# A linear attention and a gated layer on one core: w in pairs, halves summed before the column matmuls, w_out worked in place, and a new order

## The chip, the cores and the metric

The kernel runs on one core of a Trainium2 chip. The time is the device time of one execution in microseconds (us). The engines are named as the profile names them: PE (matmul) with PEld (its weight loads), DVE (vector), ACT (activation), POOL, and SP, which here only issues DMAs. Each engine takes its instructions in order.

## What is computed

The reference, cut to what matters. r, k, v, w have the shape (4, 8, 768, 48): batch, heads, steps, head size. The second part has 384 inputs and outputs and 1024 hidden columns.

```python
for t in range(S):
    cur = einsum('bhd,bhe->bhde', u * k[t], v[t])
    y[t] = einsum('bhd,bhde->bhe', r[t], state + cur)
    state = w[t][..., None] * state + einsum('bhd,bhe->bhde', k[t], v[t])
x = y.transpose(0, 2, 1, 3).reshape(B * S, H * D)
h = x @ w_in
e = exp(h - max(h)); sm = e / (sum(e) + 1e-9)
solu = h * sm
mu, var = mean(solu), mean((solu - mean(solu)) ** 2)
out = ((solu - mu) / sqrt(var + 1e-6) * g_ln) @ w_out
```

## The kernel before

The 768 steps are cut into 6 chunks of 128, and there are 4 batches, so there are 24 units of work (chunk, batch), each 128 tokens with all 8 heads. Units 0 to 3 are the first chunk. A unit goes through some thirty stages, and each stage is a small function that issues a few instructions on one engine. The text `ORDER` lists all stages of all units as words; the program goes through the words once and issues each, and a wrapper (`InOrder`) keeps every engine in that order. A word is a stage, a unit, and where there is a choice a letter: a for ACT, v for DVE, g for POOL. So `hq3a` squares for unit 3 on ACT. `ORDER` is therefore the order of PE, DVE, ACT, POOL and of SP's DMAs.

The stages by their words:

- `ldw`, `ldk`, `ldr`, `ldv`: SP loads 128x8x48 floats of an input, 192 KB in rows of 192 bytes. `ldwin`, `ldwout`, `small` load the weights and the two rows u and g_ln.
- `lw` (ACT): log of w. `cum` (PE): running sums of it, in `cum_ps`. `exp` (ACT): their exponentials in place. `et` (DVE): the decay over the whole chunk. `kp` (DVE): k and r times the decays.
- `p`, `q`, `qa`, `dg`, `dv`: the term with u: r times k, times u, summed per head (`qa` adds halves first on POOL), times v. `vb` makes v bf16.
- `kt` (PE) transposes `kp`, `kr` copies it out. `M` (PE) gives the scores in `m_ps`, `m` copies them with the mask on DVE, or without it on ACT, and then `sel` masks on POOL.
- `Y` (PE) is the attention, with the dv term added by a matmul where the word ends in x, and otherwise in `y`, which copies it out. `X` (PE) transposes y, `xT` copies. `S` (PE) and `st` (DVE) renew the state, in all but the last chunk.
- `H` (PE): the hidden layer, 24 matmuls into `h_ps`. `e` (ACT): its exponential. `he` (DVE): h times e. `hq`: the square of he.
- `Oa` and `Ob` (PE): for each of 8 hidden slices a matmul of he with `w2` (384 outputs and a column for the mean), and a matmul with one column for the sum of e; `Ob` ends with 8 one-column matmuls for the sum of hq. The last unit is worked in other parts (`Oa23`, `Ob23`, `Oc23`).
- `sq`, `qm`, `lv`, `o`, `sto`: the variance, its root, the scaled output, and the store by SP.
- `win` casts w_in. `gw` scales w_out by g_ln into `gw`, `mean` takes its mean over the hidden dimension with 8 matmuls, `mean_sb` copies it, `wt` adds it to `gw` and gives `w2`. `dm` is a matmul on zeros that only keeps PE busy.

SP issues the loads far ahead: k with r, v and w have seven buffers each. PSUM gives two large tiles (cum, m, h) and four small ones (all others).

The masks are built on POOL: `uti_neg` and `uts` by a memset and a select, `ident` and `ident_f` by a helper (masks.py in the profile). In the order in which the program issues POOL's work, those of the helper are partly behind the first `p`.

Every call of an `InOrder` engine carries line 71 in the profile, the first call of each line 68, so instructions are told apart by their tiles.

Of the kernel before, what the change touches and what calls it, by code (L numbers as in the profile page):

```python
# [24 lines left out]
dm5 dm3 dm18 dm1 ldw0 ldr0 small dm16 dm8 ldk0 lw0 ldw1 ldr1 cum0 exp0 et0 lw1 rows cum1 ldk1 p0g ldw2 kp0 exp1 ubc kt0 p1g kr0v ldr2 M0 ldk2 ldv0 et1  # L25
kp1 lw2 m0a q0g kt1 kr1v ldwin2 cum2 q1g sel0 dg0 exp2 M1 dm10 et2 vb0a kp2 m1a ldwin1 ldv1 kt2 win2a dg1 dv0g kr2v win1a vb1a Y0 y0v sel1 ldwin0 M2
win0a dm6 X0 m2v dv1v ldwout0 dm4 p2g Y1 q2g S1 y1v ldwout1 qa2 gw1a gw0a dm2 X1 xT0v xT1v dg2 H0 H1 ldw3 e0 st1 S0 dm13 ldv2 gw4v gw6v gw3g he0 ldk3
gw5a dm12 dm17 ldw4 st0 gw7a ldr3 e1 ldk4 lw3 gw2g mean mean_sb:a vb2g ldw5 dv2g he1 Y2 ldr4 cum3 wt2g y2v exp3 lw4 et3 p3v hq0a wt3g cum4 wt1g X2 dm0
wt0g ldk5 dm9 ldr5 exp4 lw5 ldw6 wt4g kp3 S2 kt3 ldv3 cum5 st2 ldw7 wt7g ldv4 et4 kr3a xT2v wt6g ldr6 Oa0 kp4 p4v exp5 wt5g M3 q3v et5 m3a kt4 kr4v
ldk6 Oa1 kp5 hq1a H2 M4 q4g kt5 Ob0 ldv5 sel3 ldw8 lw6 vb3a e2 dg3 kr5a dv3g m4v sq0a dg4 vb4g dv4g p5g vb5g Ob1 ldr7 M5 lw7 ldk7 Y3x ldv6 he2 m5v qm0  # L30
q5g p6g y3a cum6 X3 xT3v sq1v Y4 qm1 exp6 y4v H3 lv0 lv1 et6 ldr8 X4 hq2v ldk8 kp6 Oa2 dg5 o0a xT4a dv5g p7g sto0 ldw9 S4 e3 S3 st4 st3 q6g H4 Y5 vb6g
q7g ldr9 o1a he3 kt6 lw8 S5 Ob2 e4 ldk9 y5v cum7 ldr10 he4 kr6a st5 X5 hq3a sq2a exp7 M6 Oa4 ldv7 ldk10 ldr11 Oa3 qm2 m6v cum8 ldv8 qa6 et7 xT5a sto1
dg6 ldr12 ldk11 lv2 kp7 qa7 Ob3 dv6g exp8 p8g ldw10 p9v kt7 et8 o2a dg7 sq3g kp8 H5 qm3 q8g hq4a lv3 ldv9 e5 ldw11 Y6x kr7v ldv10 p10g M7 vb7g o3v Ob4
ldw12 kt8 m7v y6a q10g lw9 X6 sq4v he5 cum9 xT6a qm4 ldk12 exp9 kr8a dg8 et9 dv7g Y7 hq5g H6 e6 sto2 kp9 Oa5 ldw13 kt9 y7v lv4 X7 dg10 q9g Ob5 kr9a
he6 vb8g ldv11 ldk13 dv8g ldr13 sq5a o4a M8 ldw14 hq6g m8v S7 M9 qm5 vb10g xT7a p11g ldv12 m9v lv5 Oa6 H7 dg9 st7 lw10 Y8 o5a e7 cum10 vb9g ldw15
exp10 Ob6 y8v he7 sq6g X8 sto3 et10 dv9g S6 kp10 ldk14 xT8a lw12 S8 q11g H8 lw11 lw13 cum11 st8 e8 dv10g st6 Oa7 qm6 kt10 Y9x p12g exp11 hq7v kr10a
# [12 lines left out]
e18 he18 dv20g kt21 exp22 Ob17 kr21a M20 X19 sq17g S17 qm17 m20a lv17 kp22 qa21 sel20 lw23 S18 xT19v sto14 o17a st17 hq18g M21 Oa18 ldk23 m21v kt22
cum23 H19 sto15 st18 exp23 kr22v vb21a kp23 dg21 dv21g sto16 Y20 Y21 vb22a M22 q22g S19 e19 m22a vb23g y20v X20 p23v st19 he19 q23g Ob18 kt23 xT20a  # L50
sq18v H20 qm18 kr23a sel22 M23 y21v lv18 o18a X21 dg22 hq19v xT21v Oa19 m23a dv22v dg23 sel23 Y22 Ob19 y22v e20 he20 H21 dv23g Y23 sto17 X22 sq19a
Oa20 y23v X23 qm19 lv19 hq20g o19a xT22v e21 xT23v H22 e22 he21 Ob20 sto18 hq21g sq20a qm20 lv20 H23 he22 Oa21 Oa22 sto19 Ob21 e23 hq22g sq21a o20v
qm21 lv21 Ob22 he23 hq23v Oa23 sto20 sq22v sq23a qm22 o21v Ob23 sto21 lv22 qm23 Oc23 o22v sto22 lv23 dm14 oz23v dm15 o23a stz23 dm7 sto23 dm11 dm19
# [25 lines left out]
def kernel(  # L79
# [38 lines left out]
    def load(name, src):  # L118
        def stage(i):
            c, b = units[i]  # L120
            L = live[i]
            if name in "kr":

                if "k_and_r" not in L:
                    L["k_and_r"] = io.tile([C, 2, H, 64], F32, tag="kr_in", name="kr_in")
                t = L["k_and_r"][:, "kr".index(name)]
            else:
                t = io.tile([C, H, 64], F32, tag=name + "_in", name=name + "_in")
            L[name] = t[:, :, :D]
            sp.dma_start(out=L[name], in_=src[b, :, c * C:(c + 1) * C, :].rearrange("h t d -> t h d"))  # L130
        return stage
# [16 lines left out]
    def load_w_out(half):  # L148
# [5 lines left out]
    nc.gpsimd.memset(uti_neg, -1.0)  # L154
    nc.gpsimd.affine_select(out=uti_neg, in_=uti_neg, compare_op=ALU.is_ge, fill=0.0, base=0,
                            pattern=[[1, C]], channel_multiplier=-1)
    uts = consts.tile([C, C], BF16)
    nc.gpsimd.memset(uts, 1.0)
    nc.gpsimd.affine_select(out=uts, in_=uts, compare_op=ALU.is_gt, fill=0.0, base=0,
                            pattern=[[1, C]], channel_multiplier=-1)  # L160
    ident = consts.tile([C, C], BF16)
    make_identity(nc, ident)
# [12 lines left out]
    lw_t = [consts.tile([C, H, 64], BF16, name=f"lw{j}") for j in range(NR)]  # L175
    kp_t = [consts.tile([C, 2, H, 64], BF16, name=f"kp{j}") for j in range(NR)]
    for j in range(NR):
        nc.vector.memset(lw_t[j][:, :, D:], 0.0)
# [407 lines left out]
    def part(stage, j):  # L586
        return lambda i: stage(i, j)
# [52 lines left out]
```

The softmax here doesn't subtract the row's maximum and nothing guards it: scores larger than these inputs give would overflow.

## Time and profile before

| what | value |
|---|---|
| median of 8 runs | 151.86 us (150.96 to 155.74) |
| the profiled execution | 151.5 us, of which the span from first to last instruction is 149.8 |
| PE busy | 138.7 us, 2154 matmuls |
| DVE, ACT, POOL busy | 128.6, 119.5, 122.8 us |
| DMA | 27.09 MB, 181 GB/s on average |
| inv_col column matmuls for e | 192, row mean 165 ns |
| one_col column matmuls for hq | 192, row mean 163 ns |
| hq on POOL, on DVE, on ACT | 14 of 1892 ns, 5 of 1043, 5 of 1068 |
| lw on ACT | 24 of 523 ns |
| w_in, w_out in chunks | landing after 5.3 and 8.6 us (median) |

A row of the profile gives the mean duration of one instruction. A matmul's duration includes its way through the array, in which the next one already runs; what it adds to PE's time is the distance between two starts. Busy shares are averages over the start, the bulk and the tail, which differ.

### The profile page before, as it was taken

The numbers are of one execution on the slowest core, as the hardware profiler recorded it, in microseconds if no ns is written. First come the engines' busy times: TensorE is split into PE (matmuls) and PEld (weight loads), VectorE is DVE, ScalarE is ACT, GpSimd is POOL, SyncE is SP. The second block draws the span as 40 slices with busy tenths as digits, with TensorE's granted clock in tenths as the row PEclk, the third lists the DMA queues.
The fourth block names the chain that finished last, engine by engine and source line by source line (L and its number), as shares of the span: only waits on it lengthen the run. The fifth ranks groups of instructions, "written<-read, shape, count | busy, mean of one in ns | idle before, by whom it ended". The sixth has DMA issues, their size and how long they took to land.

```text
span 149.8 us, 5293 instructions
## 1 busy us (share of the span) xinstructions
PE 138.7 (93%) x2154; PEld 109.7 (73%) x2156; DVE 128.6 (86%) x231; ACT 119.5 (80%) x232; POOL 122.8 (82%) x152
## 2 busy tenths in 40 slices
PE   5766899599999899999999999999999999999993
PEld 2244677377886787887878888878787878888780
DVE  7545778999999998999989989988899999997661
ACT  4446939898798979799898998798999798895651
POOL 3374983999989999998988999999798989975900
PEclk9999999999999999999999999999999999999999
DMA  5999999998989998989899999996989111011113
GB/s 99 197 221 321 391 297 203 205 213 172 217 194 199 205 221 170 232 167 236 197 213 240 217 201 229 205 261 135 239 201 255 42 57 53 7 53 57 48 50 117
DMA packets 104970, 27.09 MB, mean 181 GB/s; under 512 B 100329, under 2 KB 104562, under 8 KB 104946
## 3 DMA queue, kind: packets, MB, share of 16 engines
q1 hardware_dynamic: 104946, 26.75, 78.8%
q8 instruction: 17, 0.28, 0.7%
q14 instruction: 7, 0.06, 0.1%
HBM read 22.03 MB, written 4.72 MB: 179 GB/s over the span
## 4 chain that ended last, share of the span: by engine, by line
PE 72%; DVE 11%; DMA 5%; issue 4%; ACT 4%; SPq 2%; POOL 0%; POOLq 0%; DVEq 0%; ACTq 0%
PE o_ps L71 23%; PE h_ps L71 19%; PE kr_ps L71 8%; DMA kr_in<-in_k_dram 5%; PE cum_ps L71 5%; PE y_ps L71 4%; PE m_ps L71 4%; PE s_ps L71 4%; PE x_ps L71 3%; DVE kp L71 3%; DVE p L71 2%; SPq L71 2%; DVE he L71 1%; ACT cum_ps L71 1%; DVE y L71 1%
## 5 line engine op out<-in xcount | busy, mean ns | idle before, releaser
L71 PE MATMUL o_ps<-w,he 128*128 128x385 bf16 (+2 forms) x200 | 42.3, 315 | 0.3 <-ACT sq L71 0.3
L71 PE MATMUL h_ps<-xT,win_sb 128*128 128x128 bf16 x576 | 36.3, 220 | 0.1
L71 PEld LDWEIGHTS <-win_sb 128*128 128x128 bf16 x576 | 33.3, 98 | 0.8 <-issue 0.2
L71 DVE TENSOR_TENSOR he<-h_ps,e 128x1024 bf16<-128x1024 f32 x24 | 29.2, 1217 | 3.2 <-ACT e L71 3.2
L71 PE MATMUL o_ps<-inv_col,e 128*128 128x1 bf16 x192 | 31.1, 165 | 0.0
L71 ACT ACTIVATE e<-h_ps 128x1024 bf16<-128x1024 f32 x24 | 24.5, 1022 | 7.5 <-PE h_ps L71 7.4
L71 POOL TENSOR_TENSOR hq<-he 128x1024 bf16<-128x1024 bf16 x14 | 26.5, 1892 | 3.1 <-DVE he L71 2.1
L71 PEld LDWEIGHTS <-he 128*128 128x128 bf16 x208 | 19.7, 96 | 10.5 <-issue 0.3
L71 ACT ACTIVATE cum_ps<-cum_ps 128x772 f32<-128x772 f32 (+1 forms) x24 | 19.3, 803 | 5.7 <-PE cum_ps L71 5.6
L71 DVE TENSOR_TENSOR kp<-cum_ps,kr_in 128x768 bf16<-128x768 f32 x24 | 22.7, 947 | 0.2 <-ACT cum_ps L71 0.2
L71 POOL TENSOR_TENSOR q<-p,u_bc 128x384 bf16<-128x384 bf16 x23 | 21.2, 926 | 0.7 <-DVE p L71 0.5
L71 POOL TENSOR_TENSOR dv<-vb,dg 128x384 bf16<-128x384 bf16 x22 | 18.5, 845 | 3.6 <-DVE dg L71 1.7
L71 PEld LDWEIGHTS <-kp 128*128 128x128 bf16 x272 | 17.6, 102 | 4.5 <-DVE kp L71 2.5
L71 DVE TENSOR_TENSOR m<-m_ps,uts 128x1024 bf16<-128x1024 f32 x14 | 17.0, 1221 | 2.8 <-PE m_ps L71 2.6
L71 POOL TENSOR_TENSOR p<-kr_in 128x384 bf16<-128x384 f32 x18 | 18.4, 1026 | 1.1 <-DMA kr_in<-in_k_dram 1.1
L71 PEld LDWEIGHTS <-e 128*128 128x128 bf16 x192 | 18.3, 96 | 0.1
L71 PE MATMUL kr_ps<-ident,kp 128*128 128x128 bf16 x192 | 15.9, 230 | 2.1 <-DVE kp L71 2.1
L71 ACT COPY kr<-kr_ps 128x1024 bf16<-128x1024 bf16 x13 | 13.2, 1015 | 0.8 <-PE kr_ps L71 0.8
L71 PEld LDWEIGHTS <-kr 64*128 64x128 bf16 (+1 forms) x272 | 10.5, 98 | 4.5 <-DVE kr L71 2.2
L71 ACT ACTIVATE lw<-w_in 128x384 bf16<-128x384 f32 x23 | 11.7, 523 | 0.9 <-DMA w_in<-in_w_dram 0.9
L71 POOL TENSOR_SCALAR_AFFINE_SELECT m<-m 128x1024 bf16<-128x1024 bf16 x10 | 11.0, 1100 | 1.8 <-ACT m L71 1.8
L71 PE MATMUL m_ps<-kr 64*128 64x128 bf16 x192 | 10.2, 229 | 1.7 <-DVE kr L71 1.7
(93 smaller groups left out, 280.7 us busy)
## 6 DMA issues: line engine op xcount, KB each, us to landing
w_in<-in_w_dram SPq DMA_DIRECT2D x24, 192.0 KB, 3.7
kr_in<-in_r_dram SPq DMA_DIRECT2D x24, 192.0 KB, 3.6
kr_in<-in_k_dram SPq DMA_DIRECT2D x24, 192.0 KB, 4.3
v_in<-in_v_dram SPq DMA_DIRECT2D x24, 192.0 KB, 4.4
out_dram<-o SPq DMA_DIRECT2D x23, 192.0 KB, 3.2
win_f<-in_moe_w_in_dram SPq DMA_DIRECT2D x3, 512.0 KB, 5.3
wout_f<-in_moe_w_out_dram SPq DMA_DIRECT2D x2, 768.0 KB, 8.6
out_dram<-o SPq DMA_DIRECT2D x2, 96.0 KB, 1.7
```

The lines of the kernel that those rows point to most:

```text
L71: made = make(*args, **kwargs)
```

## The change

Seven things are changed.

1. w is held in pairs of units: one tile for two, and from unit 4 on one DMA (384 KB) loads both and one activation takes the log of both. `ldw5`, `lw5` and so on are gone from the order. The first four units are loaded and worked singly.
2. `gw` writes into `w2` itself, and `wt` adds the mean to it in place; the tile `gw` is gone. The 8 matmuls of the mean are in two halves (`meanA`, `meanB`).
3. A stage `es` adds slices 4 to 7 of e to slices 0 to 3, and then the sum of e takes 4 column matmuls, not 8. It is in the order for units 16 to 22 (POOL for 18 and 19, DVE for the others).
4. A stage `hs` does the same for hq, for units 18 to 22 (POOL for 20, DVE for the others).
5. The column matmuls of e for the second half are no longer between those of `Ob` but in a stage `Oe`, for units without `es`.
6. The four masks are built by POOL in order, ahead of all its other work.
7. The order is new as a whole, and for many stages the engine. Counts: hq 8 on POOL, 3 on DVE, 13 on ACT; kr 10 on ACT, 14 on DVE (13 and 11 before); m 12 and 12 (10 and 14); xT 11 and 13 (14 and 10); sel 12 (10); qa 9 (6); dv all on POOL; gw 1 on ACT, 4 on DVE, 3 on POOL (4, 2, 2); dm 16 (20).

The diff, cut. Of the order, its beginning and its end are shown.

```diff
 ORDER = """
-dm5 dm3 dm18 dm1 ldw0 ldr0 small dm16 dm8 ldk0 lw0 ldw1 ldr1 cum0 exp0 et0 lw1 rows cum1 ldk1 p0g ldw2 kp0 exp1 ubc kt0 p1g kr0v ldr2 M0 ldk2 ldv0 et1
-kp1 lw2 m0a q0g kt1 kr1v ldwin2 cum2 q1g sel0 dg0 exp2 M1 dm10 et2 vb0a kp2 m1a ldwin1 ldv1 kt2 win2a dg1 dv0g kr2v win1a vb1a Y0 y0v sel1 ldwin0 M2
-win0a dm6 X0 m2v dv1v ldwout0 dm4 p2g Y1 q2g S1 y1v ldwout1 qa2 gw1a gw0a dm2 X1 xT0v xT1v dg2 H0 H1 ldw3 e0 st1 S0 dm13 ldv2 gw4v gw6v gw3g he0 ldk3
-gw5a dm12 dm17 ldw4 st0 gw7a ldr3 e1 ldk4 lw3 gw2g mean mean_sb:a vb2g ldw5 dv2g he1 Y2 ldr4 cum3 wt2g y2v exp3 lw4 et3 p3v hq0a wt3g cum4 wt1g X2 dm0
+dm11 dm2 dm10 dm9 dm5 dm4 ldw0 lw0 cum0 ldk0 exp0 ldr0 et0 p0g ldw1 dm6 small dm13 dm0 lw1 rows kp0 ubc ldk1 q0g cum1 kt0 dm3 exp1 ldr1 ldw2 lw2 dm7
+ldk2 kr0v ldr2 ldv0 ldwin2 M0 ldwin0 et1 kp1 kt1 m0v ldwin1 ldv1 cum2 p1g kr1a M1 dg0 exp2 ldwout0 q1g vb0v dm14 dv0g m1a Y0x et2 ldw3 kp2 kt2 p2g y0a
+kr2v win0g win2a ldwout1 q2v dm15 sel1 vb1g ldv2 dg1 M2 win1a m2a S0 X0 ldr3 xT0v dv1g H0 st0 Y1 e0 dg2 y1v ldk3 sel2 X1 S1 xT1a he0 st1 gw3g gw2g
+gw5g gw1v lw3 gw0v gw6v H1 vb2g ldw4 hq0a dv2g cum3 e1 gw4v meanA he1 gw7a exp3 ldr4 meanB ldk4 et3 Y2x S2 ldv3 mean_sb:a wt3g kp3 ldr5 hq1a kt3 y2a
+p3v wt0g X2 wt2g lw4 ldk5 kr3v M3 wt1g cum4 wt7v q3v st2 ldv4 ldw6 m3a wt4g wt5g cum5 Oa0 wt6g Oa1 exp4 p4v exp5 et4 xT2a kp4 q4v et5 kt4 kp5 H2 ldr6
...
-Oa20 y23v X23 qm19 lv19 hq20g o19a xT22v e21 xT23v H22 e22 he21 Ob20 sto18 hq21g sq20a qm20 lv20 H23 he22 Oa21 Oa22 sto19 Ob21 e23 hq22g sq21a o20v
-qm21 lv21 Ob22 he23 hq23v Oa23 sto20 sq22v sq23a qm22 o21v Ob23 sto21 lv22 qm23 Oc23 o22v sto22 lv23 dm14 oz23v dm15 o23a stz23 dm7 sto23 dm11 dm19
+es20v xT22a hs19v lv18 Y23 H22 e21 y23v hq20g X23 he21 xT23v Ob19 o18a e22 he22 sq19a qm19 Oa20 hs20g es21v H23 lv19 o19a e23 Ob20 hq21v es22v Oa21
+sq20g hq22a qm20 Oa22 lv20 hs21v sto17 o20a Ob21 sq21v he23 hs22v hq23v Ob22 qm21 sq22v Oa23 sto18 sto19 lv21 sto20 qm22 sq23a Ob23 o21v lv22 qm23
+lv23 sto21 Oc23 o22v o23v sto22 oz23a dm12 stz23 dm1 dm8 sto23
 """
...
+            elif name == "w":
+                if i % 2 == 0:
+                    t2 = io.tile([C, 2, H, 64], F32, tag="w_in", name="w_in", bufs=4)
+                    for a in range(2):
+                        live[i + a]["w2_in"] = t2
+                        live[i + a]["w"] = t2[:, a, :, :D]
+                if i >= 4:
+                    sp.dma_start(out=L["w2_in"].rearrange("t a h d -> t (a h) d")[:, :, :D],
+                                 in_=src[b:b + 2, :, c * C:(c + 1) * C, :].rearrange("b h t d -> t (b h) d"))
+                else:
+                    sp.dma_start(out=L["w"], in_=src[b, :, c * C:(c + 1) * C, :].rearrange("h t d -> t h d"))
+                return
...
-    make_identity(nc, ident)
+    ident_f = consts.tile([KF, KF], F32)
+    for t, value, keep, fill in ((uti_neg, -1.0, ALU.is_ge, 0.0), (ident, 0.0, ALU.not_equal, 1.0),
+                                 (uts, 1.0, ALU.is_gt, 0.0), (ident_f, 0.0, ALU.not_equal, 1.0)):
+        pool.memset(t, value)
+        pool.affine_select(out=t, in_=t, compare_op=keep, fill=fill, base=0,
+                           pattern=[[1, t.shape[1]]], channel_multiplier=-1)
...
-            act.activation(out=gw[:, f, :], in_=wout_f[:, f, :], func=COPY, scale=gr[:, f:f + 1])
+            act.activation(out=w2[:, f, :DM], in_=wout_f[:, f, :], func=COPY, scale=gr[:, f:f + 1])
...
-        engine.tensor_add(out=w2[:, f, :DM], in0=gw[:, f, :], in1=mean_sb)
+        engine.tensor_add(out=w2[:, f, :DM], in0=w2[:, f, :DM], in1=mean_sb)
...
     def log_w(i):
-        L = live[i]
-        L["lw"] = lw_t[i % NR]
-        act.activation(out=L["lw"][:, :, :D], in_=L["w"], func=LN)
+        t = lw_t[i // 2 % (NR // 2)]
+        both = range(i, i + 2) if i >= 4 else range(i, i + 1)
+        for j in both:
+            live[j]["lw"] = t[:, j % 2]
+        if len(both) == 2:
+            act.activation(out=t.rearrange("t a h d -> t (a h) d")[:, :, :D],
+                           in_=live[i]["w2_in"].rearrange("t a h d -> t (a h) d")[:, :, :D], func=LN)
+        else:
+            act.activation(out=live[i]["lw"][:, :, :D], in_=live[i]["w"], func=LN)
...
-            pe.matmul(o_ps[:, DM + 1:DM + 2], lhsT=e[:, f, :], rhs=inv_col, start=False, stop=False,
-                      skip_group_check=True)
+            if part == 0:
+                sum_of_e(i, f)
         if part == 1:
-            for f in range(KF):
-                pe.matmul(o_ps[:, DM + 2:], lhsT=L["hq"][:, f, :], rhs=one_col, start=False, stop=(f == KF - 1),
+            hq = L.get("hs", L["hq"])
+            n = hq.shape[1]
+            for f in range(n):
+                pe.matmul(o_ps[:, DM + 2:], lhsT=hq[:, f, :], rhs=one_col, start=False, stop=(f == n - 1),
                           skip_group_check=True)
+    def sum_of_e(i, f):
+        L = live[i]
+        pe.matmul(L["o_ps"][:, DM + 1:DM + 2], lhsT=L.get("es", L["e"])[:, f, :], rhs=inv_col, start=False, stop=False,
+                  skip_group_check=True)
+    def output_e(i):
+        for f in range(KF // 2, KF):
+            sum_of_e(i, f)
+    def halves(name, of):
+        def stage(i, engine):
+            L = live[i]
+            t = L[name] = wk.tile([128, KF // 2, C], BF16, tag=name, name=name, bufs=2)
+            engine.tensor_add(out=t, in0=L[of][:, :KF // 2, :], in1=L[of][:, KF // 2:, :])
+        return stage
```

## The prediction

> **What bounds the kernel now.** I read the page's busy line first, then the windows by stage, the chain of waits, and the timeline where the chain leaves TensorE.
>
> ```profile
> span 149.8 us, 5293 instructions
> PE 138.7 (93%) x2154; PEld 109.7 (73%) x2156; DVE 128.6 (86%) x231; ACT 119.5 (80%) x232; POOL 122.8 (82%) x152
> DMA  5999999998989998989899999996989111011113
> PE 72%; DVE 11%; DMA 5%; issue 4%; ACT 4%; SPq 2%; POOL 0%; POOLq 0%; DVEq 0%; ACTq 0%
> ```
>
> Four engines above 80% and a chain that lies 72% on PE: PE bounds the bulk, and the others follow closely. DMA is full until about 105 us of the span, so inputs can matter early and not late.
>
> ```profile
> 0.00:32.80 32.80, 25.25 (x242) 16.84 (x245) 24.18 (x67) 21.92 (x31) 21.70 (x34) 1.00 0.98 240
> 32.80:57.00 24.20, 23.54 (x404) 19.40 (x402) 23.53 (x38) 20.72 (x43) 23.11 (x31) 1.00 0.99 201
> 57.00:110.00 53.00, 53.00 (x903) 43.51 (x902) 48.67 (x81) 47.53 (x98) 49.96 (x61) 1.00 0.97 210
> 110.00:138.90 28.90, 28.66 (x498) 23.91 (x496) 26.83 (x41) 24.41 (x46) 24.81 (x28) 1.00 0.33 84
> ```
>
> These windows (columns: PE, PEld, DVE, ACT, POOL busy, clock, DMA share, GB/s) are cut at the hidden block of unit 2 (32.8 us) and of unit 23 (138.9). Before 32.8 PE issued 242 matmuls in 32.8 us; afterwards 17 per us. So there are two stores of time: the start-up, and PE's own work. DVE has 7.1 us idle between 32.8 and 138.9 (106.1 less 23.53 + 48.67 + 26.83).
>
> What a small matmul really costs is read from starts, not from durations:
>
> ```profile
> 80.26 0.32 PE L71 MATMUL o_ps<-w,he 128*128 128x385 bf16 x1
> 80.42 0.16 PE L71 MATMUL o_ps<-inv_col,e 128*128 128x1 bf16 x1
> 80.45 0.33 PE L71 MATMUL o_ps<-w,he 128*128 128x385 bf16 x1
> ...
> 81.02 0.34 PE L71 MATMUL o_ps<-one_col,hq 128*128 128x1 bf16 x8
> 81.22 0.33 PE L71 MATMUL x_ps<-ident,y 128*128 128x128 bf16 x3
> ```
>
> The e column starts at 80.42, the next matmul at 80.45: 0.026 us, not the 0.165 of its row. Eight hq columns take 81.02 to 81.22: 0.025 each. Summed in this way, the start-to-start gaps beyond each kind's median are 7.5 us after 32.8.
>
> The start-up, in the merged chain (start, us, what), and two lines of the timeline:
>
> ```profile
> 18.59 0.76 DVE dv L71
> 19.45 0.57 DVE y L71
> 20.06 0.50 PE x_ps L71 x3
> 20.56 3.02 PE h_ps L71 x48
> ```
>
> ```profile
> 7.02 0.29 POOL masks.py:199 TENSOR_SCALAR_AFFINE_SELECT ident<-ident 128x128 bf16<-128x128 bf16 x1
> 8.47 1.01 PE L71 MATMUL kr_ps<-ident,kp 128*128 128x128 bf16 x8
> ```
>
> The first hidden block stands behind y and x of unit **1**, although only its own x and w_in are needed; the mask of `ident` waits in POOL's queue behind the first p, which waits for k.
>
> **What the Trainium skill says.** "TensorE: Matmul & The Clock Gate", section "Wait — 56ns, not 53.3ns?": start-to-start never falls below about 25 ns however small N is; the trace agrees (0.025). The same page, "What's actually happening": PE runs at half rate until a window of about 3.4 us was busy; here the hidden block's matmuls start 0.107 us apart until 21.1 us and 0.056 after. "SBUF — State Buffer", "Who interferes with whom": a DVE instruction with two SBUF inputs contends with a GpSimd one that reads SBUF, and the loser blocks. The trace agrees: hq on DVE took 0.69 us at 142.81, when POOL was done, and 1.17 as the median of five.
>
> **The change, part by part.**
>
> *Half sums.* Seven `es` and five `hs` stages each replace eight column matmuls by four: 12 x 4 = 48 matmuls fewer, at 0.025 to 0.027: **-1.25 us of PE**, nearly all on the path, since the units concerned (16 to 22) run where PE has 28.66 of 28.90 us. Each needs an addition of 128x512. No row shows one. Five es and four hs lie on DVE: half of hq's 0.69 to 1.45 us is 0.35 to 0.73; I take 0.5. Three lie on POOL at half of 1.89, 0.95. A late sum stops PE, which issues in order; behind it wait Ob and all later units.
>
> *Masks first.* On POOL the other masks move up too, past nothing but p, before which POOL idled 4.17 us for k. ident is ready near 2.2 us rather than 7.3. Alone this would move the transposes from 8.47 to kp's end, 6.97. But the new order puts three warm-ups (0.43 each) and the rows (1.6) between the first cum and the second: 4.9 + 1.3 + 1.9 + 0.8 = 8.9. I cost it at **0** (-1.5 to +0.4): what covers it is that filling, which keeps PE busy from 1.5 to 10 us and may release the clock before 10.
>
> *New start.* X0 and H0 now precede Y1 on PE. w_in's last part, moved ahead of v1, should land near 17.0 (before 17.7); its cast is 1.05, so H0 starts at 18.2 to 18.5 instead of 20.4. H1 needs sel1, vb1 and dv1 on POOL behind the cast of win0 (about 1.3, by vb's 0.503 for 384 columns): 21.3 instead of 22.1. What the end feels is H2. It is behind kt4, kp4, r4 and k4. SP's queue up to k4 now holds two loads more (w5, r4), and a load takes 0.9 us of a full DMA: k4, landed at 27.1, lands at 28.9; then kp4 0.95 and transposes 0.45 give H2 at 30.4; PE's work between H1 and H2 (6 us from 22.7) does not forbid that. With slips of 0.6, H2 at 31.0: **-1.8 us** (0 to -2.5). The next loads (v3 three places earlier, k5 near 31.7, w6 with w7 near 34.4, then 0.9 each) stay ahead of their users.
>
> *w in pairs.* SP issues 14 loads of w instead of 24, with the same bytes and the same rows of 192 bytes: no DMA time. A pair's log has 768 elements; exp of 768 took 0.80, and "ScalarE: Activation LUTs", "What ACT_TABLE_LOAD costs", gives 186 ns + 0.833 a element = 0.83 (for 384: 0.51; the trace has 0.52). ACT: 24 x 0.523 becomes 4 x 0.523 + 10 x 0.82: -2.25. The even unit waits for both halves, a load more; w has 1 to 2 us of slack for units 4 to 7, and cum4 then starts about 28.1 instead of 27.6, before k4 is there, so hidden.
>
> *w_out in place, mean in halves.* Same matmuls (8 of 0.163), same additions, seven of them on POOL and one on DVE; POOL's solid 7.8 us from 26.3 is broken up. Cost nothing: it ends where Oa0 starts, about 29.5 to 30.4, as before; were it later, PE would lack Oa0's 0.76.
>
> *Work moved between engines*, count by row mean. ACT: hq +8 x 1.07, m +2 x 1.02, o +3 x 0.58; kr -3 x 1.02, gw -3 x 0.61, vb -3 x 0.51, xT -3 x 0.48, win -1.05, lw -2.25, qm -0.8: **+0.4**. POOL: hq -6 x 1.89, q -2 x 0.93, wt -1.0, qm -0.7; half sums +2.9, qa +3 x 1.04, sel +2 x 1.1, dv +2 x 0.85, gw, win, p, vb +4.6: **-0.4**. DVE: half sums +4.5, kr +3 x 0.68, xT +3 x 0.35, gw +2 x 0.53, q +2 x 1.06, rest +1.6; m -2 x 1.22, hq -2 x 1.04, p -1.2, dv -2 x 0.65, o -3 x 0.61, dg -0.9: **+2.7** (+1.4 to +4.8). DVE's 7.1 us of idle covers it in sum but not in every place: I give **+0.6** back (0 to +2). Four warm-ups fewer: nothing, two are in the tail beside the last stores, two in idle time.
>
> *Tail.* After H23 PE now has Ob20, Oa21, Oa22, Ob21, Ob22 (about 3.8 us) before the last unit, against Oa21 to Ob22 (3.4): 0.4 later from H23, which comes 0.4 earlier for having less ahead of it. e23, he23, hs22 and hq23 chain to about the same point. Zero.
>
> **Sum:** 151.5 (this execution's own time; span 149.8 and 1.7 around it) - 1.25 - 1.8 + 0.6 = 149.05. The median of the runs is 0.36 above it: **149.4**.
>
> **Rivals.** A measurement here tells about 0.5% (0.76 us) from no change.
>
> (a) *Everything fits*: an early clock, start-up at its best (-2.5), no giving back, and an idle us or so filled of the 7.5: 151.86 - 1.25 - 2.5 - 0.7 = 147.4. For it: at most hidden blocks the new order has 1 to 2 us less PE work ahead of the block. Against: a chain between engines never fits perfectly. 15%.
>
> (b) *Start-up given back to DMA*: H2 stays at 32.8 because loads land no earlier; only the columns count: 151.86 - 1.25 + 0.6 = 151.2. For it: DMA at 0.98 of the first 32.8 us. Against: the loads before H2 leave 2 us. 19%.
>
> (c) *DVE becomes the bound, slower*: place, units 16 to 23, where the half sums, y, kr and he share DVE. If DVE needs its present idle time for hand-overs, added work lengthens the stage: 151.86 - 1.8 + 2.7 = 152.8 at my price, 154.9 at 4.8. It decides once more than 2.5 us of added DVE time finds no gap. For it: DVE's 93% from 32.8 to 138.9, and that two-input instructions stretch beside POOL (p took 1.82 us at 113.6). Against: POOL loses six of its 1.89 us squares, which held it longest. 21%.
>
> That the sums don't shorten PE's list is excluded by the instruction lists: PE has 52 pairs of load and matmul less, 48 and four warm-ups.
>
> **Numbers.** My forecast (148.3 to 150.5) has 45%. Range 146.6 to 153.2: it takes in (a) but its edge, (b), and (c) to just over its lower price. Faster 0.65 (forecast, (a), a third of (b)), same 0.14, slower 0.21.
>
> **What would show it.** H0 near 18.4, H2 near 31.0; 2102 matmuls; DVE busy near 131, half sums near 0.5; PE gaps after H2 no more than 8 us. Wrong, if H2 is at 32.8 or later, if PE waits on DVE in the last 40 us, or if half sums exceed 0.7.

## The result and the profile after

The changed kernel takes 154.76 us in the median of 11 runs (153.33 to 156.41); before took 151.57 in the median of 32. The ratio is 1.0187, with a 95% interval of 1.0157 to 1.0217: slower by 1.9%. The forecast was 149.4 us and the range ended at 153.2. The profiled execution of the changed kernel took 154.66 us. (Some executions of every version here are several us longer than its others; the times given below are medians of all, the ratios leave those out.)

The lines of the page that answer to those of before:

```profile
span 152.9 us, 5199 instructions
PE 138.0 (90%) x2103; PEld 107.5 (70%) x2104; DVE 131.7 (86%) x246; ACT 121.2 (79%) x219; POOL 121.9 (80%) x158
```

PE has lost 51 matmuls and a little busy time, and its share fell from 93% to 90%. DVE rose by 3.1 us. The span grew by as much.

The windows, cut at the hidden blocks of unit 2 (now at 32.9 us) and unit 23 (now at 141.6), with the same columns as before (length, PE, PEld, DVE, ACT, POOL busy, clock, DMA share, GB/s):

```profile
0.00:32.90 32.90, 25.63 (x242) 15.80 (x244) 24.86 (x66) 21.50 (x29) 23.01 (x35) 1.00 0.99 240
32.90:57.00 24.10, 22.89 (x391) 18.66 (x388) 20.87 (x40) 21.16 (x39) 21.00 (x26) 1.00 0.91 182
57.00:110.00 53.00, 51.59 (x886) 42.76 (x884) 48.75 (x86) 46.29 (x84) 49.47 (x70) 1.00 0.99 212
110.00:141.60 31.60, 29.85 (x489) 24.35 (x486) 30.81 (x45) 25.90 (x50) 27.88 (x28) 1.00 0.29 81
```

H2 starts where it did before, so the start gave nothing. By hidden blocks, the 3.2 us more of the span are 0.1 up to H2, -0.2 from H2 to H8, 0.6 from H8 to H16, 2.2 from H16 to H23 and 0.5 after it. From 110 us to H23 the stage takes 31.6 us where it took 28.9 (0.5 of that because H16 came later), although PE has nine matmuls fewer in it. DVE is busy for 30.81 of 31.60 us there (98%, before 93%), and PE for 29.85 of 31.60 (94%, before 99%). In this last third DVE sets the pace.

Summed as in the prediction, PE's start-to-start gaps after H2 are about 11.5 us, against 7.5 before. Four of them are over 0.5 us: 1.07 at 53.9 (ahead of X6), 1.06 at 75.9, 0.63 at 115.6 and 1.13 at 138.7 (ahead of X23). The account of the profiled pair is then roughly: 0.1 for H2, 4.0 more gaps, 1.3 less matmul work (PE's list valued at each kind's usual distance of starts, against the same order without half sums), so 2.8 of the 3.1 us.

The half sums, from the answers for the tiles es and hs (minimum, median, maximum in ns; first and last start):

```profile
L72 DVE TENSOR_TENSOR es<-e x5: 407/414/1404, 114.0 to 143.2; 128x512 bf16<-128x512 bf16 x5
L72 DVE TENSOR_TENSOR hs<-hq x4: 410/834/2115, 132.4 to 145.4; 128x512 bf16<-128x512 bf16 x4
```

One takes 0.41 us when it runs freely. The nine on DVE took 8.04 us in all, because four of them took 1.40, 1.22, 1.25 and 2.12. What those four have in common is seen by putting DVE and POOL side by side (start, us, what), here for two of them:

```profile
113.96 1.40 DVE L72 TENSOR_TENSOR es<-e 128x512 bf16<-128x512 bf16 x1
113.99 1.10 POOL L72 TENSOR_SCALAR_AFFINE_SELECT m<-m 128x1024 bf16<-128x1024 bf16 x1
...
137.14 1.94 POOL L72 TENSOR_TENSOR hq<-he 128x1024 bf16<-128x1024 bf16 x1 [0.30 <-DVE he L72]
137.25 2.12 DVE L72 TENSOR_TENSOR hs<-hq 128x512 bf16<-128x512 bf16 x1
139.28 0.55 DVE L72 TENSOR_TENSOR y<-y_ps,dv 128x384 bf16<-128x384 f32 x1
```

es ends at 115.36, 0.27 after the select; hs ends at 139.37, 0.29 after POOL's square. The other two end in the same way, 0.28 and 0.27 after POOL's instruction. Each waits until POOL is done and then needs some 0.3 us. Behind the second one on DVE stands y23, for which PE waits ahead of X23: the 1.13 us.

### The profile page after: what moved, and what is told of

Its sections match the earlier page's. It is cut to its first block, busy times and chain, and to the rows that moved or that the text cites. A ratio compares the mean times of both kernels' runs of the same rounds, so it can differ in the third digit from the quotient of the medians.

```text
span 152.9 us, 5199 instructions
## 1 busy us (share of the span) xinstructions
PE 138.0 (90%) x2103; PEld 107.5 (70%) x2104; DVE 131.7 (86%) x246; ACT 121.2 (79%) x219; POOL 121.9 (80%) x158
## 5 line engine op out<-in xcount | busy, mean ns | idle before, releaser
L72 PE MATMUL o_ps<-w,he 128*128 128x385 bf16 (+2 forms) x200 | 40.1, 316 | 1.2 <-DVE st L72 0.9
L72 PE MATMUL h_ps<-xT,win_sb 128*128 128x128 bf16 x576 | 36.1, 219 | 1.6 <-DVE xT L72 0.9
L72 PEld LDWEIGHTS <-win_sb 128*128 128x128 bf16 x576 | 32.8, 98 | 2.6 <-ACT win_sb L72 1.0
L72 POOL TENSOR_TENSOR p<-kr_in 128x384 bf16<-128x384 f32 x20 | 20.5, 1028 | 5.5 <-DMA kr_in<-in_r_dram 5.5
L72 PEld LDWEIGHTS <-he 128*128 128x128 bf16 x208 | 18.5, 97 | 8.8 <-issue 0.3
L72 DVE TENSOR_TENSOR m<-m_ps,uts 128x1024 bf16<-128x1024 f32 x12 | 14.6, 1217 | 1.8 <-PE m_ps L72 1.8
L72 POOL TENSOR_TENSOR hq<-he 128x1024 bf16<-128x1024 bf16 x8 | 15.2, 1900 | 0.9 <-DVE he L72 0.9
L72 PE MATMUL o_ps<-inv_col,e 128*128 128x1 bf16 x136 | 15.0, 165 | 0.0
L72 ACT ACTIVATE hq<-he 128x1024 bf16<-128x1024 bf16 x13 | 13.7, 1054 | 0.1
L72 POOL TENSOR_SCALAR_AFFINE_SELECT m<-m 128x1024 bf16<-128x1024 bf16 x12 | 13.1, 1091 | 0.6 <-ACT m L72 0.6
L72 DVE TENSOR_TENSOR y<-y_ps,dv 128x384 bf16<-128x384 f32 x19 | 10.4, 551 | 3.4 <-POOL dv L72 1.4
L72 ACT CAST m<-m_ps 128x1024 bf16<-128x1024 f32 x12 | 12.1, 1010 | 1.1 <-PE m_ps L72 1.1
L72 ACT COPY kr<-kr_ps 128x1024 bf16<-128x1024 bf16 x10 | 10.1, 1014 | 3.4 <-PE kr_ps L72 3.4
```

The source lines that it names most:

```text
L72: made = make(*args, **kwargs)
```

## Experiments

Ratios are to before on the same chip, with 95% intervals.

**a1, the new order without half sums.** All `es` and `hs` words are gone and `Oe` is back for units 16 to 22.

```diff
-es16v es17v es18g es19g es20v es21v es22v hs18v hs19v hs20g hs21v hs22v
+Oe16 ... Oe22   (each ahead of its Ob)
```

> The changed kernel without the half sums: es and hs are gone for units 16 to 22, and PE takes all 8 columns again (48 matmuls more, 1.25 us of PE). Theory L (each half sum on DVE is held by a POOL instruction and holds up y, kr and kp behind it): faster than the changed kernel by 1.5 to 3 us, near 152.3, and PE's 1.1 us gap before the x of the last unit is gone. Rival O (the loss comes from the new order before unit 16, and the half sums pay by themselves): slower than the changed kernel by 0.5 to 1.25 us, near 155.5.

Measured: 154.15 us, 1.014 (1.004 to 1.024). The gap ahead of X23 is gone, the one near 76 stays (at 77.5 here), and the gaps after this trace's own H2 (36.0) are about 8 us. In the medians most of the loss is there without the half sums; the interval is too wide to split it by this run alone. The traces split it better: from H16 to the end takes 42.8 us here, 43.8 in the changed kernel and 41.1 in before. In this stretch the half sums take 1.3 us from PE's list and add some 2.2 us of gaps, so they cost about 1.0 us.

**a2, half sums alone in the order of before** (w_out in place too, to make room).

```diff
-he16
+he16 es16v   (likewise 17v, 18g, 19g, 20v, 21v, 22v)
-Ob18
+hs18v Ob18   (likewise 19v, 20g, 21v, 22v)
```

> The kernel before, in its own order, with half sums for the same units on the same engines (es behind he, hs ahead of Ob), and w_out in place, which makes room for their tiles. Theory L: no gain, 0 to 2 us slower than before (151.6 to 153.6), with some half sums on DVE over 1 us. Rival O: faster than before by up to 1.2 us, near 150.5.

Measured: 158.82 us, 1.035 (1.030 to 1.041). H18 is still at 118.7 us, 0.5 after before's; then PE waits ahead of the sums over hs, 1.74 us at 129.6, and again at 135.6 and from 145 us on. On DVE hs took up to 2.11 us. Where I put them they hurt far more than in the new order, which had been arranged around them.

**a3, r8 loaded earlier.** In the changed kernel r8 was issued at 43.66 and landed at 49.15; kp8 and p8 waited, and through dv6 and y6 the gap of 1.07 at 53.9 arose.

```diff
-ldk8 ... hq2g ... ldr8
+ldk8 ldr8
```

> The changed kernel with one load moved: r of unit 8 directly behind k of unit 8, three loads earlier. In the changed kernel it landed at 49.15, kp8 on DVE and p8 on POOL waited for it, then dv6, y6, and PE stood 1.07 us. Theory D (this late load costs what PE stood): 1.0 to 1.5 us faster than the changed kernel, near 153.5. Rival (the gap comes back later, since other engines are behind as well): under 0.4 us, near 154.6.

Measured: 155.76 us, 1.021 (1.004 to 1.039). The gaps at 49.8 and 53.9 are gone, and yet H6 and H8 start at 56.7 and 64.5 us, where they were (56.8, 64.6). That trace's own start was later (H2 at 34.4), so the gap's worth is not cleanly told; no gain is shown. Nor is it shown that the edit removed the gap: the traces of a1, a4, c2 and d2, which leave r8 where it was, do not have it either.

**a4, y23 ahead of es20 and hs19 on DVE.**

```diff
-es20v xT22a hs19v lv18 Y23 H22 e21 y23v
+xT22a lv18 Y23 H22 e21 y23v es20v hs19v
```

> The changed kernel with two words moved: y of unit 23 on DVE goes ahead of es20 and hs19. Theory L: hs19 took 2.12 us and y23 stood behind it, so PE's gap of 1.13 us before the x of unit 23 goes: 0.8 to 1.1 us faster than the changed kernel, near 153.8. Rival: hs19 is still held by the square on POOL and Ob19 waits for it, so the gap only moves: under 0.3 us, near 154.6.

Measured: 155.15 us, 1.0195 (1.013 to 1.026). The timeline of DVE after it:

```profile
137.53 1.16 DVE L72 TENSOR_TENSOR es<-e 128x512 bf16<-128x512 bf16 x1
138.61 1.37 DVE L72 TENSOR_TENSOR hs<-hq 128x512 bf16<-128x512 bf16 x1
```

Both are held, and PE now waits 1.08 us at 138.8 for the sum over hs. The wait moved and kept its size: on a full DVE, order does not remove the 2.5 us that these two take instead of 0.8.

**b5, s1, s2: which part of the change, which third of the order?** b5 is the changed kernel's code without half sums in the order of before. s1 and s2 are spliced: one order up to H16, the rest in the other.

```diff
-ORDER of the changed kernel, without es and hs
+b5: ORDER of before, with pairs of w, meanA meanB and Oe
+s1: ORDER of before up to H16, then what is left in the new order
+s2: the new order up to H16, then what is left in ORDER of before
```

> The changed kernel's code (masks first, w in pairs of units, w_out in place) under the order of before, and no half sums. Theory (what the change loses without its half sums is the new order): these three edits cost nothing, 151.2 to 152.4 us, within 0.5% of before, and H0, H2, H8 and H16 start within 0.5 us of before's 20.4, 32.8, 64.7 and 108.7. Rival (the pairs or the masks cost, because a pair of logs of 0.83 us holds ACT at once and its 384 KB lands late): 153.5 to 154.3 us, as the new order without half sums, which took 1.4% more than before.

> The same code without half sums; the order of before up to H16, and what is then left in the order of the changed kernel. Theory (the new order loses in its last third: H16 to the end of the span took 42.8 us in the new order without half sums and 41.1 in before): H16 near 108.7 and some 1.5 us more than before, 153.2 to 153.8 us. Rival (the loss is in the start and the middle, and the last third is longer only because of what it inherits): within 0.5% of before, 151.3 to 152.5 us.

> The same code without half sums; the order of the changed kernel up to H16, and what is then left in the order of before. Theory (the loss is in the last third): H16 at 109.2 to 109.7, 0.5 to 1 us after before's, and the last third takes before's 41.1 us: 152.2 to 152.8 us. Rival (start and middle): 153.5 to 154.3 us.

Measured: b5 155.54 us, 1.011 (1.006 to 1.016); s1 156.45, 1.027 (1.022 to 1.032); s2 155.33, 1.019 (1.013 to 1.025). Both splices are worse than or as bad as either whole order: each has a seam of its own (in s2 PE waits 1.33 us near 100, ahead of a cum, for he on DVE). They do not tell which third loses. b5 was not level with before, against my theory; the three executions that its ratio counts lie at 153.6 to 153.7 us, in the rival's range, and H2 came at 34.4. Its profiled execution had something new: hq13 on DVE took 4.12 us, where before has 0.68. That led to the next two runs.

**c3, the hold by itself.** Appended to the kernel before: four instructions of one kind on DVE, first alone, then beside three POOL instructions in a row.

```diff
+    for mine, theirs in ((two, None), (one, None), (from_psum, None), (two, g_mul), (one, g_mul),
+                         (from_psum, g_mul), (two, g_select)):
+        ...
+        if theirs is not None:
+            for n in range(3): theirs()
+        for n in range(4): mine()
```

> The kernel before with a tail of its own appended after the last store's operands are ready, so only the trace of that tail counts and the time is longer by it: four operations of one kind on DVE by themselves (bf16 sum of two halves, 128x512, SBUF to SBUF; bf16 copy of one half; product of f32 PSUM and bf16 SBUF), then each kind beside three 128x1024 bf16 products back to back on POOL (1.9 us each), and the half sum beside three selects on POOL (1.09 us each). Theory (a DVE instruction that reads two bf16 tiles of SBUF cannot run while a POOL instruction does, and a run of POOL instructions without a gap holds it to the run's end): the half sum takes 0.41 us alone and one of the four is held for most of the 5.7 us run, 3.5 to 5.7 us; copy and PSUM product are not held, within 20% of their time alone. Rival (the two only share bandwidth): each of the four half sums takes 0.6 to 1.2 us beside POOL, and the copy is stretched as well.

The answers for the tile, one stage after the other: half sum, copy and PSUM product alone; then half sum, copy and PSUM product beside POOL's products; then the half sum beside selects.

```profile
L71 DVE TENSOR_TENSOR lk_d<-lk_e x4: 416/424/426, 148.5 to 149.9; 128x512 bf16<-128x512 bf16 x4
L71 DVE COPY lk_d<-lk_e x4: 282/294/295, 151.2 to 152.2; 128x512 bf16<-128x512 bf16 x4
L71 DVE TENSOR_TENSOR lk_d<-lk_ps,lk_e x4: 681/692/692, 153.3 to 155.5; 128x512 bf16<-128x512 f32 x4
...
L71 DVE TENSOR_TENSOR lk_d<-lk_e x4: 425/1998/2022, 157.0 to 163.1; 128x512 bf16<-128x512 bf16 x4
L71 DVE COPY lk_d<-lk_e x4: 294/1913/1937, 164.2 to 170.0; 128x512 bf16<-128x512 bf16 x4
L71 DVE TENSOR_TENSOR lk_d<-lk_ps,lk_e x4: 681/691/691, 170.9 to 173.1; 128x512 bf16<-128x512 f32 x4
...
L71 DVE TENSOR_TENSOR lk_d<-lk_e x4: 424/1193/1210, 177.2 to 180.9; 128x512 bf16<-128x512 bf16 x4
```

Beside POOL's products of 1.9 us three of four half sums take 2.0 us, and the fourth, when POOL is done, 0.42. Beside selects of 1.1 us they take 1.2. The product that reads PSUM and one tile of SBUF is not touched. So it is a wait for one POOL instruction, not a sharing of bandwidth. Two things in my theory were wrong: the hold ended with each POOL instruction and not with the run of three, and the copy from SBUF to SBUF is held just as the sum is. The Trainium skill, "SBUF — State Buffer", section "Who interferes with whom", says both: the one that comes first keeps the shared ports for its whole instruction, and a copy can need them too. The trace agrees with 2.0 against 0.42 us and 1.9 against 0.29.

**c1, b5 with hq13 on ACT.**

```diff
-hq13v
+hq13a
```

> The order of before in the changed kernel's code (masks first, pairs of w, w_out in place, no half sums), and hq13 on ACT instead of DVE, where it took 4.04 us beside a run of POOL instructions without a gap (0.68 in before, where POOL had a gap of 0.31 us). Theory (that hold of 3.4 us is what the pairs and masks cost in this order, by shifting the instant): 151.3 to 152.7 us, and H14 to H15 takes 7.4 to 8.5 us instead of 11.8. Rival (pairs and masks cost by their loads and by the longer log, at the start): 153 to 154 us, with H2 still at 33.8 to 34.4.

Measured: 153.6 us, 1.016 (1.013 to 1.020). The hold is gone and H14 to H15 takes 7.5 us, as in before. But the theory fails, and both numbers of the rival came true: 153 to 154 us, and H2 at 34.2. The trace is 2.5 us longer than that of before. About half of it is new: on ACT hq13 takes 1.06 us ahead of xT14, and PE waits 1.16 us for that ahead of H14. The other half is the start, where H2 is 1.45 us later. There PE waits for the log ahead of cum4, which is now that of a pair (before, then c1):

```profile
27.62 0.32 PE L71 MATMUL cum_ps<-lw,uti_neg 128*128 128x384 bf16 x1 [1.31 <-ACT lw L71]
```

```profile
28.23 0.48 PE L72 MATMUL cum_ps<-lw,uti_neg 128*128 128x384 bf16 x1 [2.03 <-ACT lw L72]
```

Beside the longer wait the matmuls take 0.48 us instead of 0.32; the granted clock is 0.52 from 28.0 to 31.5 us. b5 and s1 have the same stretch (0.51 for 3.5 us, waits of 1.70 and 1.91, H2 at 34.4 and 33.8). The traces with early masks and single logs (d1: wait 1.31, H2 at 33.1) and with pairs and the old masks (b1 and e3: wait 1.63, H2 at 32.7 and 32.1) do not. So in these traces neither early masks nor pairs alone make the start of this order late.

**d1, masks first alone** (and w_out in place), in the order of before.

```diff
-    make_identity(nc, ident)
...
-    make_identity(nc, ident_f)
+    the four masks in one loop of memset and affine_select, ahead of POOL's other work
```

> The kernel before with the masks first (all four built on POOL from 0.79 to 2.67 us, ahead of p0, where before built ident and ident_f after it, to 7.44 us) and w_out in place; single w, its own order and sums. Theory (with this order, the earlier masks let units 0 to 2 run about 1 us earlier, and that is lost again behind the loads of k3 and k4, with a later H2): H0 at 19.3 to 19.6 us, H2 at 33.8 to 34.4 instead of 32.8, and 0.5% to 1% over before. Rival (masks are worth nothing, and the late H2 of the two earlier runs with before's order comes from the pair of w4 and w5 ahead of k4): H2 at 32.6 to 33.2 us and a time within 0.3% of before.

Measured: 153.0 us beside 152.89 of before, 1.0004 (0.9974 to 1.0035). The masks cost nothing and bring nothing, although H0 comes at 19.6 instead of 20.4; H2 is at 33.1. The profiled execution of d1 took 158.69 us, and in it hq13 was held again. First DVE and POOL of before, then of d1:

```profile
95.70 0.68 DVE L71 TENSOR_TENSOR hq<-he 128x1024 bf16<-128x1024 bf16 x1
95.85 1.21 POOL L71 TENSOR_TENSOR dv<-vb,dg 128x384 bf16<-128x384 bf16 x1 [0.31 <-DMA out_dram<-o]
```

```profile
98.46 0.91 POOL L71 TENSOR_TENSOR q<-p,u_bc 128x384 bf16<-128x384 bf16 x1
98.51 4.10 DVE L71 TENSOR_TENSOR hq<-he 128x1024 bf16<-128x1024 bf16 x1
99.32 0.83 POOL L71 TENSOR_TENSOR dv<-vb,dg 128x384 bf16<-128x384 bf16 x1
100.11 1.95 POOL L71 TENSOR_TENSOR p<-kr_in 128x384 bf16<-128x384 f32 x2
102.14 2.11 POOL L71 TENSOR_TENSOR q<-p,u_bc 128x384 bf16<-128x384 bf16 x2
```

In before, hq13 begins in a gap of 0.31 us in which POOL waits, and it is dv that takes 1.21 instead of 0.83. In d1 it begins 0.05 us after q and is held through q, dv and two p, until 102.06, when POOL pauses for 0.08 us. b5 (4.12 us) and s1 (4.12) are the same, with the same four POOL instructions. So where the instruction falls against POOL's decides over 3.4 us. The rule quoted under c3, one whole instruction, does not cover this; why these four were not parted after the first, as in c3, the runs don't show.

**b4, exp4 ahead of m3.** To test what holds H2 in the changed kernel.

```diff
-m3a ... exp4 p4v exp5 et4 xT2a kp4
+exp4 ... et4 kp4 ... m3a
```

> The changed kernel with its half sums; only the start of the order differs: cum4 ahead of M3 on TensorE, exp4, et4 and kp4 ahead of m3a, st2 and p4v. Theory (what gates H2 is exp4, which stood at 30.37 us on ACT behind m3a of 1.01 us, and not k4, which had landed at 29.04): kp4 starts 1 us or more earlier, at 30.0 to 30.4, and H2 at 31.7 to 32.3 us instead of 32.9; but H6 to H8 come no earlier than 56.5 and 64.3, since loads pace them, so that the time moves by less than 0.5 us, 154.3 to 155.0. Rival (the start is worth its full size at the end): 153.6 to 154.0 us.

Measured: 156.2 us, 1.025 (1.019 to 1.030). The changed kernel and b4 in the part that matters (ACT and DVE of the first, then ACT and PE of the second):

```profile
29.46 1.01 ACT L72 CAST m<-m_ps 128x1024 bf16<-128x1024 f32 x1 [0.52 <-PE m_ps L72]
30.37 1.61 ACT L72 ACTIVATE cum_ps<-cum_ps 128x772 f32<-128x772 f32 x2
31.33 0.94 DVE L72 TENSOR_TENSOR kp<-cum_ps,kr_in 128x768 bf16<-128x768 f32 x1
```

```profile
30.02 0.80 ACT L72 ACTIVATE cum_ps<-cum_ps 128x772 f32<-128x772 f32 x1 [0.71 <-PE cum_ps L72]
30.73 1.02 ACT L72 CAST m<-m_ps 128x1024 bf16<-128x1024 f32 x1
31.80 0.48 PE L72 MATMUL cum_ps<-lw,uti_neg 128*128 128x384 bf16 x1 [1.55 <-ACT m L72]
```

In the changed kernel kp4 waits for exp4, and exp4 stands behind m3. Put first, exp4 makes m3 late, which keeps one of the two large PSUM tiles, and PE, which is in order, waits 1.55 us for it ahead of cum5. kp4 starts at 30.9, only 0.4 earlier, and H2 comes at 36.1 us. The wait is half of that delay; after it the matmuls of this trace are slower too (0.48 us where the changed kernel has 0.32, granted clock 0.50 from 32 to 37 us). The gate has two sides and my edit only changed sides.

**c2, st10 ahead of m11, without half sums.** PE's gap of 1.06 near 76 is in every trace of the new order so far: the next output needs a small PSUM tile, which the state matrix of unit 10 gives back when st10 has read it.

```diff
-m11v S10 st10
+S10 st10 m11v
```

> The new order without half sums (154.2 us, 1.4% over before), with S10 and st10 ahead of m11 on DVE: TensorE had stood for 1.06 us near 76 in every run of the new order, since the small PSUM tile of the next output waited for st10 behind m11's 1.22 us. Theory (the gap is on the path): it goes, and with it 0.7 to 1.1 us, 153.1 to 153.6 us. Rival (m11 is late next): a gap of 0.6 to 1.1 us ahead of Y11 or X11 in its place, 154.0 to 154.5 us.

DVE in the changed kernel:

```profile
75.26 1.23 DVE L72 TENSOR_TENSOR m<-m_ps,uts 128x1024 bf16<-128x1024 f32 x1
76.40 0.55 DVE L72 TENSOR_TENSOR st<-s_ps,et 128x384 bf16<-128x384 f32 x1
```

Measured: 152.92 us, 1.0075 (1.004 to 1.011), where a1 had 1.014; the two intervals overlap. In c2's trace st10 starts at 76.16, ahead of m11. Of the gap 0.37 us is left, and a wait of 0.21 follows it. From H8 to H16 the trace takes 44.1 us (so do those of d3 and e1, which have the same edit), where a1's takes 44.6. So the theory holds in direction; the traces show 0.5 us, half of the gap, and the ratios alone cannot tell that from the whole.

**d2, the same with the half sums.**

```diff
-m11v S10 st10
+S10 st10 m11v      (in the changed kernel)
```

> The changed kernel with its half sums, S10 and st10 ahead of m11 on DVE. With the same kernel without half sums at 1.0075 of before, this prices the half sums in the new order. Theory (held by POOL, they cost more than their 48 matmuls of 0.026 us bring): 1.011 to 1.015 of before, TensorE's gap near 76 gone and the ones behind half sums (ahead of kr17 and of X23) still there. Rival (without that gap they pay): 1.000 to 1.005.

Measured: 154.69 us, 1.0128 (1.006 to 1.019). Against the changed kernel that is again 0.6% for st10, but its trace takes 44.6 us from H8 to H16, as the changed kernel's does, so no gain of st10 is shown with the half sums in. Against c2 it prices the half sums: 0.5%, as does the pair of 1.0187 and a1's 1.014. Each difference alone is within its intervals; they agree with each other and in sign with a2, and the traces agree (H16 to the end: 43.4 us, in c2 42.8). The gap ahead of X23 (1.13 at 137.8) is there as expected; the one ahead of kr17 is 0.46.

**b1 and e3, pairs of w alone** (with w_out in place), in the order of before, and **e2, w_out in place alone.**

```diff
-ldw4 lw4 ... ldw5 lw5
+ldw4 lw4      (384 KB and one log for both; likewise 6, 8, ... 22)
```

> The kernel before with w and its log in pairs, and w_out in place; its own masks, order and sums. Theory (nothing but a shift of instants): H2 at 32.6 to 33.2 us, as before; the time is before's if hq13 on DVE keeps clear of POOL's run, 151.3 to 152.5, and 153.5 to 155 if it is held as in the order of before with masks first; the trace's hq13 tells which. Rival (w5's 192 KB ahead of k4 delays the start by itself): H2 at 34 us or more and 153 us or more with hq13 at 0.7 us.

> Pairs and in place under the order of before a second time, for its trace: the first trace had the span of before, 149.8 us, while its other executions lay in two groups, 151.2 to 151.5 and 152.3 to 153.2 us. Theory (the upper group loses at the start, where the clock of TensorE was granted lower and loads land later): a trace of the upper group has H2 at 33.5 to 34.2 us and from there on the times of the first. Rival (it loses late, at a half that is held by POOL): H2 near 32.7 and a single gap of 1 us or more later.

> The kernel before with w_out scaled and centred in place, nothing else. It splits the 1.006 of in-place plus pairs. Theory (pairs cost, in place nothing): 0.998 to 1.002. Rival (the centring, which now rewrites the tile that the mean was read from, delays the start): 1.004 to 1.008.

Measured: b1 152.42 us, 1.006 (1.003 to 1.009); e3, the same kernel again, 151.96, 1.0036 (1.0011 to 1.0061); e2 151.66, 1.0018 (0.9994 to 1.0042). In place costs nothing. Pairs cost 0.2 to 0.4% over it, about what can be told. The traces of b1 and e3 both have the span of before (149.8, 149.6) with H2 at 32.7 and 32.1; an execution of b1's upper group, 152.3 to 153.2 us, was not caught, so where it loses is not shown. The record gives a hint: b1's six executions below 151.5 us all have a granted clock of 1.00 on average, and nine of its eleven others 0.94 to 0.99 (in e3 two of nine below 151.9, seven of ten above). A stretch at the lower clock, as in c1, would fit.

**d3, the new order with the old masks**, and **e1, with single loads and logs of w** (both without half sums, st10 first).

```diff
-ldw4 ... lw4
+e1: ldw4 ldw5 ... lw4 lw5      (each two next to each other; likewise 6 to 22)
+d3: ident and ident_f by make_identity, as in before
```

> The new order without half sums, S10 and st10 ahead of m11, and the masks built as in before (ident and ident_f late). Theory (the order is paced by loads at its start, so that early masks bring nothing): H2 as in the new order with masks first, 32.9 to 36 us, and 1.004 to 1.010 of before. Rival (masks first cost as such): 0.996 to 1.002.

> The new order without half sums, st10 ahead of m11, and w loaded and its log taken one unit at a time, each two right after each other where the pair stood. Theory (what the new order still has over before, 0.75%, comes with the pairs, as pairs alone under the order of before took 1.006): 0.999 to 1.003 of before. Rival (single loads add ten DMA issues of about 0.6 us on SP and some 2.3 us of work on ACT, and the rest of the loss is the new order's): 1.006 to 1.012.

Measured: d3 153.77 us, 1.0085 (1.005 to 1.012); e1 152.82, 1.0059 (1.003 to 1.008). Neither can be told from c2 (1.0075). What is left of the loss belongs to the new order itself; no part of it is shown for masks or pairs.

## Why the prediction was wrong

The loss of 1.9%, taken apart by the ratios: half sums 0.5% (1.0187 to 1.014, and 1.0128 to 1.0075), the wait behind st10 0.6% (1.014 to 1.0075, and 1.0187 to 1.0128), the rest of the new order 0.6 to 0.85% (c2, d3, e1). Only for the last do the intervals leave zero out. The traces give 0.6 to 1.0 us for the half sums and at most 0.5 us for st10. Masks and in place are zero, as forecast (d1, e2). After H2 the prediction had -0.65 us (-1.25 and +0.6) and the trace has +3.0; up to H2 it had -1.8 and the trace has +0.1. Point by point:

- **Column matmuls, -1.25 us: held.** 51 matmuls fewer in the trace, 48 of them these; PE's list, worked out from start distances, is 1.3 us shorter than that of a1.
- **The half sum at 0.5 us: the term that was mis-sized.** Free, it is 0.41, so even less than I took; in place it averaged 8.04 / 9 = 0.89, and at worst 2.12. I read half of hq's 0.69 to 1.45 as the range. But a held instruction does not scale with its own size: it takes the rest of POOL's instruction, whatever its length. I quoted the rule, had 1.17 against 0.69 in the trace, and still priced by elements. "Wrong if half sums exceed 0.7" was the right test, and it was met.
- **DVE +2.7 us of work, of which 0.6 comes back: failed.** DVE's total was right (131.7, forecast near 131), but the average hid the place. Between 110 us and H23 it has 3.98 us more than before in that stage, and only 2.07 of idle time had been there. That is rival (c), in its place; its price of 152.8 in the sum supposed that the start pays 1.8, which it did not. That its upper price, 154.9, is near the measured 154.76 is luck: it had DVE at +4.8 and the start at -1.8, and they were +3.1 and +0.1.
- **Start-up, -1.8 us: failed.** H0 came at 19.0 and H1 at 22.3, later than the 18.2 to 18.5 and 21.3 forecast, and H2 at 32.9. k4 landed at 29.04, as worked out (28.9). But k4 was not what kp4 waited for: exp4 was, 31.2 at its end, behind m3 on ACT (p4 on DVE, ahead of kp4, ended at 31.3 as well). And exp4 could not have run much earlier, since cum4 started at 29.4: I had it at 28.1 and called it hidden, but the pair's log ran from 28.1 to 28.9. I had followed the loads to H2 and the queue of ACT not at all. Over the ten traces of the new order (the changed kernel, a1, a3, a4, b4, c2, d2, d3, e1, s2) H2 lies between 31.7 and 36.1 us; over those of the order of before with its own masks it is 32.1 to 32.8. So the new start is not faster, and it spreads more. The spread goes with the speed of PE ahead of H2, for which my forecast of H2 had no term. In the changed kernel, d2, d3, e1 and s2 the 24 matmuls of H1 start 0.056 us apart, and H2 comes at 31.7 to 33.9; in a1, a3, a4 and c2 they start 0.105 apart, and H2 comes at 34.4 to 36.0. b4, the latest, has its stretch at the lower clock after H1. H1 in the changed kernel, then in a1:

```profile
22.32 1.50 PE L72 MATMUL h_ps<-xT,win_sb 128*128 128x128 bf16 x24 [0.40 <-ACT xT L72]
```

```profile
24.56 2.72 PE L72 MATMUL h_ps<-xT,win_sb 128*128 128x128 bf16 x24 [0.25 <-ACT xT L72]
```

Why executions of one order differ in this, the runs don't show.
- **Middle, costed at nothing: failed.** The gap near 76 (small PSUM tile, st10 behind m11) was not among my parts at all. For every stage moved, one has to ask what PSUM tile it gives back and who waits for it. r8's late landing was of this kind too: its DMA stood behind k8, whose issue took 3.54 us, and a3 shows no gain from mending it. From H8 to H16 the trace takes 44.6 us, before 44.0, although PE has less to do there.
- **Pairs, no DMA time: nearly held.** A pair's log takes 0.834 us (forecast 0.82); the cost of pairs is 0.2 to 0.4% in the order of before and none that can be told in the new one. In the order of before the pair lengthens PE's wait for the log ahead of cum4, 1.63 us in b1 and e3 where before has 1.31.
- **Masks, zero: held.** The first transposes came at 8.7 us (forecast 8.9, a sum in which one term, 1.9, is not explained by the 1.6 given for the rows).
- **Tail, zero: roughly held.** H23 to the end takes 11.4 us, before 10.9: about the 0.4 that was forecast for the longer list. Whether 0.4 came back ahead of H23 cannot be seen behind the 2.7 by which H23 was late.

Open is where the remaining 0.6 to 0.85% of the new order goes; the traces narrow it. From H16 to the end the order of before takes 41.1 to 41.2 us in seven traces without half sums (before, b1, b5, c1, d1, e2, e3), the new order without half sums 42.6 to 42.8 in all four (a1, c2, d3, e1). That is not waiting: PE's gaps in this stretch are 2.6 us in before and 2.2 to 2.5 in those four. The new order leaves PE 22 more matmuls for it (651 against 629 in the traces, warm-ups apart). So it has to be 1.6 us ahead at H16 to be level, and in c2, d3 and e1 it gets there at 109.2, 108.1 and 107.7, where before has 108.7. What is missing is lost ahead of H16, in different places: c2 and d3 have a late H2 (34.9 and 33.8), e1 an early one (31.7) and then gaps of 0.82 at 35.4 and 0.90 at 53.1. No version here beats before.

## What to carry to other kernels

Price an added DVE instruction between SBUF tiles by what POOL does at that moment: either its own time, or the rest of POOL's instruction. Look at the stage where it goes for idle time, not at the whole span, and where POOL is as busy as here, leave PE the small matmuls it can hide at 0.026 us each. When an order is rewritten, follow for each critical block every queue that feeds it (loads, ACT, and the PSUM tiles that are given back), since the first one checked need not be the last to arrive. And before reading a wait into the difference of two starts, compare the distance of the same matmuls in both traces.

## What the hardware showed that I had not expected

- A copy of 128x512 bf16 from SBUF to SBUF on DVE, with a single input, is held by POOL like a sum (1.9 us instead of 0.29), while a product that reads PSUM is not (0.69 both times).
- A hold can span several POOL instructions: 4.10 to 4.12 us through four of them in three traces, and in each until POOL paused for less than 0.1 us. The same instruction took 0.68 us in before. It was seen only in three executions that lie 2.8 to 5.7 us over the median of their kernel (b5, s1, d1), so it bears on none of the ratios; what shifts the instruction against POOL there is not shown.
- Matmuls of one kind start 0.105 us apart in one execution and 0.056 in another of nearly the same order, in the same stage (H1, above), and a stretch of some 3.5 us at half the granted clock came back at 28 us beside waits of 1.7 to 2.0 us (b5, c1, s1), and not beside waits of 1.3 to 1.6 us (before, b1, d1, e3).
